# Row loads of k and v, a conv along the free axis, and a 128-row first transform stage in a two-headed SSM kernel

## The chip, the cores and the metric

The kernel runs on one core of one Trainium2 chip. The time is what the device needs for one execution, in microseconds; of several runs the median is given. The engines are named as in the profile: PE (TensorE matmul; PEld its weight loads), DVE (VectorE), ACT (ScalarE), POOL (GpSimd) and SP (SyncE, which issues most DMAs). Each engine takes its instructions in the order in which they stand in its own stream.

## The reference

Two sequence mixers over 2048 steps, with 640 channels each, stand side by side in the output. A is a diagonal complex state-space model, B a gated long convolution.

```python
# A: per step t
Lam_bar = exp(dt * Lam);  B_bar = ((Lam_bar - 1) / Lam)[:, None] * Bmat
h = Lam_bar * h + x[t] @ B_bar.T
y = 2 * (hs @ Cmat.T).real + x * Dskip
# B
k_shift = sum(k_pad[:, t:t+S] * shift_k[:, 3 - t] for t in range(4))   # causal, 4 taps
kv = k_shift * v
y = irfft(rfft(kv, 4096) * rfft(ssm_k, 4096))[:2048] + kv * ssm_D
out_B = q * y
out = concat([out_A, out_B])          # (1, 2048, 1280), bfloat16
```

## The kernel before

Everything lives in one SBUF arena of 128 partitions (class `Layout` gives each named part its columns; parts are reused in time) and in eight PSUM banks. `build` (L947) describes the program as a list of operations with the arena columns that each reads and writes; `Program.depend` makes dependencies of these. The order of the work is not found at run time: the string `ORDER` (L1050) holds one entry per operation, its number, the letter of its engine (T = PE, A = ACT, V = DVE, G = POOL, S = SP) and its PSUM bank. So an operation such as an eviction, an addition or a scaling that could run on several engines runs on the one that its entry names, and a wait holds up all that stands behind it on that engine. The numbers of the operations are given out in the order of `build`, so a change of the program gives all entries new numbers.

Part A works on time cut into 16 residues (i) of 128 steps (s). The *up* sweep (`up2`, `up1`, `up0`, matmuls at L554 through `base` and L575 through `rmm`) multiplies transposed x (`load_x`, L522, eight DMA transposes) with transposed B (`load_B`, L489) and combines residues in a tree; it is evicted at L571, L595 and L620. `coarse` (L646 to L660, names cs_...) runs the scan over the 128 coarse steps. `scale_C` (gC, L544, evicted at L548) scales the output matrix. `down` (dn, L677 and L679, evicted and added at L695 or L697, names ad...) distributes the states: where the addition runs on DVE it is a tensor addition of PSUM and SBUF, where it runs on ACT, PE adds the old value with an identity matmul first (L677) and ACT only copies. `project` (C, L714) makes the output: it loads the rows of x (L705), multiplies them with Dskip (xd, L706), adds the product in PSUM (ev_C, L716) and stores (st_A, L720). In these names the digits behind a stage are the unit, for instance the level and the first channel block.

Part B is a transform of length 4096 in two stages, on half of the channels (hf 0 or 1, 320 channels) at a time. Time is split in 32 coarse steps a and 64 fine steps b; the partitions hold (e, a), with four groups e of 80 channels. The filter ssm_k is h, its load `load_h` (L762) and `addD` (L764, which adds ssm_D into the filter's first column, for which a small load of ssm_D, ld_D, must have landed). The first stage `s1` (L832, evicted at L837, names e1...) has ten units of eight channel columns for h and for k, per half: each 64-row half of the partitions is multiplied by the table F1, in tiles of 64 rows by 64 columns, four at a time. The second stage `s2` (L850, evicted at L863, e2...) multiplies with the table W. `product` (L874 to L881; pp, pq, py, pz) multiplies the two spectra; `r2` (L895, L900) and `r1` (L916, and L928, which multiplies with q) transform back; `store` (L940) writes out. `tables_G` (L327, L329; g_q, g_s, g_k) makes the table for `r1`.

What k and v go through before the first stage is this. `load_kv` (L769) loads k and v of 128 channels by a DMA transpose each, with channels on the partitions and time along the free axis, five times (d = 0 to 4). `conv` multiplies the shifted k with a scalar per partition (cm, four times, by the helper at L197 or L198, on DVE or ACT), adds (ca, L795, three times) and multiplies with v (cx, L796). `plane` (L802) spills the result to a DRAM tensor, kv_rows, and `relay` (L812) reloads it with (e, a) on the partitions, four DMAs per half, each in runs of 64 elements. `setup` fills the tables: F1 at L271; `load_small` loads the four shift weights of each channel (L745).

The call of the first stage, for column i of a unit, half b of the table and half l of the rows:

```python
e.matmul(B[64 * b:64 * b + 64, 512 * l + 64 * i:512 * l + 64 * i + 64], lhsT=lh[i][ps], rhs=F[ps, b, :], start=True,
         stop=True, tile_position=(64 * l, 64 * b))
```

## Time and profile before

| | us |
|---|---|
| median of 3 runs (206.31 to 207.75) | 206.9 |
| span of the profiled execution | 205.6 |
| first matmul of the up sweep | 10.67 |
| mean granted TensorE clock | 0.970 of full speed |

In the profile a row of grouped instructions reads: line, engine, operation, what it writes and reads, the shapes, the count; then the busy time in us and the mean of one in ns; then the idle time of the engine in front of them, and what ended it. A row of a stretch reads: its bounds, its length, the busy time of each engine with the number of instructions in brackets, the granted clock, the share of the 16 DMA engines that was busy, and what they moved. A row of a wait reads: who waited, for whom, how long in all, how often, the longest. A row in order of time reads: start, length, engine, line, operation, count. A busy PE is not a PE at its peak: the end of a matmul is modelled, and two that overlap are one busy stretch. A DMA share can read a little over 1.

The DMA queues took 77.4% of the time of the 16 engines, in 107226 packets of 29.35 MB, nearly all of them under 512 bytes. The DMAs that the change is about, KB each and median us from issue to landing (none where the landing isn't seen):

```profile
arena<-in_B_ssm_k_dram SPq DMA_DIRECT2D x8, 320.0 KB, 7.1
kv_rows<-arena SPq DMA_DIRECT2D x5, 512.0 KB, 4.2
arena<-in_B_k_dram SPq DMA_TRANSPOSE x5, 5.7
arena<-in_B_v_dram SPq DMA_TRANSPOSE x5
```

### The profile page before, as it was taken

To read this page: it belongs to the slowest core of one execution; us is meant where nothing else is said; L and a number is where in the kernel's file an instruction comes from. 1 tells how busy PE (TensorE), PEld (TensorE's weight loads), DVE (VectorE), ACT (ScalarE), POOL (GpSimd) and SP (SyncE) were. 2 spreads that over 40 slices of the span, in tenths; PEclk is the share of its full clock that TensorE was granted. 3 is DMA by queue.
4 is the path that set the end of the run, shared out by engine and by line. 5 is a ranking of instruction groups with operands and counts; after the bars stand their busy time and mean duration, and the time that the engine had idled before them with its cause. 6 is when DMAs were issued, how large, how long until landed. Compare 5 with 4: busy or idle time off the path is not lost.

```text
span 205.6 us, 8247 instructions
## 1 busy us (share of the span) xinstructions
PE 180.7 (88%) x3713; PEld 118.7 (58%) x3713; DVE 166.2 (81%) x228; ACT 142.5 (69%) x164; POOL 76.4 (37%) x63
## 2 busy tenths in 40 slices
PE   2399999999999989768759999999999998999891
PEld 0245444554556647447546757546577776887670
DVE  4929349798949698798697989999999899988821
ACT  2628897887994889999738799996999950550000
POOL 8799900000040727037310180684910507120120
PEclk9999999999999999999965899999999999999998
DMA  4999979989999989659948990140962794166866
GB/s 124 160 195 168 183 163 168 136 187 156 228 222 180 267 135 199 109 100 129 134 141 171 161 101 3 40 129 3 212 80 67 171 218 96 66 160 168 227 165 156
DMA packets 107549, 30.20 MB, mean 147 GB/s; under 512 B 102394, under 2 KB 106874, under 8 KB 107514
## 3 DMA queue, kind: packets, MB, share of 16 engines
q1 hardware_dynamic: 107226, 29.35, 77.4%
q8 instruction: 29, 0.48, 1.1%
q10 hardware_dynamic: 288, 0.33, 0.5%
q14 instruction: 6, 0.05, 0.1%
HBM read 10.99 MB, written 7.86 MB: 92 GB/s over the span
## 4 chain that ended last, share of the span: by engine, by line
PE 46%; ACT 24%; DVE 10%; DMA 10%; issue 5%; POOL 1%; SPq 0%; DVEq 0%; ACTq 0%
PE acc L714 14%; PE acc L554 12%; ACT arena L863 8%; ACT arena L837 7%; DMA arena<-in_B_k_dram 6%; PE acc L850 5%; PE acc L679 3%; PE acc L832 3%; PE acc L895 3%; DVE arena L716 2%; PE acc L575 2%; DVE arena L874 2%; ACT arena L198 2%; DVE arena L877 2%; PE acc L916 2%
## 5 line engine op out<-in xcount | busy, mean ns | idle before, releaser
L554 PE MATMUL acc<-arena 128*64 128x512 bf16 x400 | 50.0, 403 | 3.9 <-issue 3.6
L714 PE MATMUL acc<-arena 128*128 128x320 bf16 x320 | 46.0, 300 | 1.4 <-DVE arena L716 0.8
L554 PEld LDWEIGHTS <-arena 128*64 128x64 bf16 x400 | 23.4, 112 | 26.5 <-issue 6.5
L714 PEld LDWEIGHTS <-arena 128*128 128x128 bf16 x320 | 30.4, 98 | 14.4 <-issue 0.9
L837 ACT CAST arena<-acc 128x1024 bf16<-128x1024 f32 x34 | 32.7, 1033 | 5.8 <-PE acc L832 5.6
L863 ACT CAST arena<-acc 128x960 bf16<-128x960 f32 (+1 forms) x37 | 32.5, 907 | 5.7 <-PE acc L850 4.9
L850 PE MATMUL acc<-arena 128*64 128x160 bf16 x512 | 23.2, 238 | 2.5 <-ACT arena L863 1.3
L832 PE MATMUL acc<-arena 64*64 64x64 bf16 x1280 | 18.2, 205 | 6.9 <-ACT arena L837 3.0
L706 POOL TENSOR_TENSOR arena<-arena 128x640 bf16<-128x640 bf16 x9 | 13.4, 1499 | 28.0 <-DMA arena<-in_A_x_dram 28.0
L850 PEld LDWEIGHTS <-arena 128*64 128x64 bf16 x512 | 18.2, 111 | 8.8 <-ACT arena L863 3.7
L900 ACT CAST arena<-acc 128x1024 bf16<-128x1024 f32 x16 | 15.5, 1021 | 10.8 <-PE acc L895 10.8
L832 PEld LDWEIGHTS <-arena 64*64 64x64 bf16 x1280 | 14.5, 117 | 14.0 <-ACT arena L837 6.2
L795 DVE TENSOR_TENSOR arena<-arena 128x2048 bf16<-128x2048 bf16 x14 | 17.8, 1268 | 5.8 <-ACT arena L198 5.5
L198 ACT ACTIVATE arena<-arena 128x2048 bf16<-128x2048 bf16 (+3 forms) x15 | 18.6, 1243 | 5.4 <-DMA arena<-in_B_k_dram 4.2
L697 DVE TENSOR_TENSOR arena<-acc,arena 128x1024 bf16<-128x1024 f32 (+2 forms) x17 | 19.2, 1148 | 1.4 <-ACT arena L863 0.7
L881 POOL TENSOR_TENSOR arena<-arena 128x1280 bf16<-128x1280 bf16 x3 | 8.5, 2821 | 27.5 <-DVE arena L877 27.5
L716 DVE TENSOR_TENSOR arena<-acc,arena 128x640 bf16<-128x640 f32 x16 | 13.3, 832 | 4.9 <-PE acc L714 4.8
L434 POOL TENSOR_TENSOR arena<-arena 128x1280 bf16<-128x1280 bf16 x1 | 2.3, 2331 | 32.1 <-ACT arena L198 32.1
L679 PE MATMUL acc<-arena 128*128 128x512 bf16 (+2 forms) x50 | 13.0, 346 | 0.6 <-ACT arena L837 0.5
L197 DVE TENSOR_SCALAR arena<-arena 128x2048 bf16<-128x2048 bf16 (+2 forms) x17 | 11.8, 699 | 1.2 <-DMA arena<-in_B_k_dram 0.9
L928 DVE TENSOR_TENSOR arena<-acc,arena 128x960 bf16<-128x960 f32 (+1 forms) x12 | 11.9, 1040 | 0.7 <-DMA arena<-in_B_q_dram 0.4
L874 DVE TENSOR_TENSOR arena<-arena 128x2560 bf16<-128x2560 bf16 x8 | 11.9, 1486 | 0.1
(139 smaller groups left out, 269.1 us busy)
## 6 DMA issues: line engine op xcount, KB each, us to landing
out_dram<-arena SPq DMA_DIRECT2D x32, 160.0 KB, 3.1
arena<-in_B_ssm_k_dram SPq DMA_DIRECT2D x8, 320.0 KB, 7.1
kv_rows<-arena SPq DMA_DIRECT2D x5, 512.0 KB, 4.2
arena<-kv_rows SPq DMA_DIRECT2D x8, 320.0 KB, 5.6
arena<-in_A_x_dram SPq DMA_DIRECT2D x16, 160.0 KB, 4.2
arena<-in_B_q_dram SPq DMA_DIRECT2D x8, 320.0 KB, 5.7
arena<-in_A_B_im_dram ACTq DMA_DIRECT2D x1, 160.0 KB
arena<-in_A_B_re_dram ACTq DMA_DIRECT2D x1, 160.0 KB, 2.7
```

Of the source, the lines that this page charges most:

```text
L198: self.SM = {nc.scalar: lambda out, in_, by: nc.scalar.mul(out, in_, by), nc.vector: vm(nc.vector), nc.gpsimd: vm(nc.gpsimd)}
L554: e.matmul(o[64 * r:64 * r + 64], lhsT=self.BT[j][:, r, d, :], rhs=self.XP[:, d, 2 * q:2 * q + 2], start=(d == 0), stop=(d == 4), skip_gro ...
L679: e.matmul(B[:, o:o + 128 * k], lhsT=c.RR[:, n, j, :], rhs=A[:, j, q:q + k, 0:128], start=not by_pe, stop=True, skip_group_check=True)
L697: e.tensor_tensor(out=o, in0=b, in1=o, op=ALU.add)
L714: e.matmul(B[:, 512 * b:512 * b + 320], lhsT=lh[j], rhs=self.CT[:, j, 320 * b:320 * b + 320], start=(j == 0), stop=(j == 9))
L716: P.add(f"ev_C{i}", {PDVE: dve(640)}, lambda e, B: e.tensor_tensor(out=ys.rearrange("p (b n) -> p b n", b=2), in0=B.rearrange("p (b n) -> ...
L795: P.add(f"ca{d}_{j}", tt, lambda e: e.tensor_tensor(out=t1, in0=t1, in1=t2, op=ALU.add), outs=[t1], ins=[t1, t2])
L832: e.matmul(B[64 * b:64 * b + 64, 512 * l + 64 * i:512 * l + 64 * i + 64], lhsT=lh[i][ps], rhs=F[ps, b, :], start=True, stop=True, tile_pos ...
L837: P.add(f"e1{what}{hf}_{u}", {PACT: act(1024), PDVE: dve(1024)}, lambda e, B: c.CP[e](out=out, in_=B.rearrange("p (l n k s) -> p k s l n", ...
L850: e.matmul(B[64 * s:64 * s + 64, 512 * b + 160 * i:512 * b + 160 * i + 160], lhsT=c.W[:, k, 64 * b:64 * b + 64], rhs=self.AS[hf][:, k, 160 ...
L863: c.CP[e](out=out, in_=b.rearrange("p r (k j n) -> p r k j n", k=n, j=4) if nj > 1 else b.rearrange("p r (k x) -> p r k x", k=n))
L874: P.add(f"pp{hf}", n1, lambda e: e.tensor_tensor(out=pt, in0=X, in1=Yk, op=ALU.mult), outs=[pt], ins=[X, Yk])
```

## The change

k and v of one half are loaded directly, 16 DMAs in all, with (e, a) on the partitions and, along the free axis, 64 time steps b of 80 channels: runs of 160 bytes. One buffer K, with 240 columns in front for the three time steps before, and the one buffer KV, which v is loaded into, serve both halves. DMA transposes of k and v, kv_rows, `plane` and `relay` are gone. The conv now shifts k by whole rows of 80 columns; the three earlier time steps that lie in another partition are fetched by one matmul with a shift matrix SH (hl) and one copy (ev_hl) per half. The weight of a tap is no longer a scalar per partition but a row of 80 values, repeated over 32 time steps, so each tap is a tensor by tensor multiplication, of 2560 columns, twice per half. The weights are loaded four times over all partitions (ld_sk) and rearranged (sw). The first stage takes all 128 rows at once: F1 has four slots of which one per partition group is filled (me4), and a unit is 16 matmuls of 128 rows with 128 columns, in two column tiles. Three parameter loads and the weight loads stand on ACT's queue. Some parts of the arena move.

```diff
-for _name, _n in (..., ("Y", 10240), ("T", 6656), ("KT", 2064), ("VT", 6144), ("H0", 5120), ("KV", 5120), ..., ("F1", 128), ...
+for _name, _n in (..., ("Y", 10240), ("T", 2560), ("TT", 5120), ("K", 5360), ("KV", 5120), ("H0", 5120), ..., ("F1", 256), ...
...
+    P.add("iota_sh", {G: .3}, lambda e: e.iota(SH, pattern=[[1, 128]], base=-1, channel_multiplier=-1, ...
+    P.add("sh", {V: .2}, lambda e: e.tensor_single_scalar(out=SH, in_=SH, scalar=0.0, op=ALU.is_equal), outs=[SH], ins=[SH])
+    edge = SH.rearrange("p (e a) -> p e a", a=32)[:, :, 0:1]
+    P.add("shz", {V: .1, G: .2}, lambda e: e.memset(edge, 0.0), outs=[edge])
...
+    P.add("me4", {V: .12}, lambda e: e.tensor_tensor(out=me4, in0=io4, in1=bc(pe_i, [128, 4]), op=ALU.is_equal), ...
-        out=F1.rearrange("p (k s) -> p k s", s=2), in0=bc(..., [128, 64, 2]), in1=bc(me..., [128, 64, 2]), op=ALU.mult)
+        out=F1.rearrange("p (k s) -> p k s", s=4), in0=bc(..., [128, 64, 4]), in1=bc(me4..., [128, 64, 4]), op=ALU.mult)
...
-        P.add("ld_par", {PSP: .1}, ...
+        P.add("ld_par", {PSP: .1, PACT: .1}, ...
...
+        for x in range(4):
+            rows = raw[32 * x:32 * x + 32]
+            P.add("ld_sk", {PSP: .4, PACT: .4}, lambda e, x=x, rows=rows: e.dma_start(
+                out=rows.rearrange("p (h y) -> p h y", h=2), in_=bass.AP(ssk.tensor, 320 * x, [[0, 32], [1280, 2], [1, 320]])), ...
...
-    def load_kv(self, d):
-        for n, out, x in (("k", c.v("KT", 16, 2048), self.k2), ("v", c.v("VT", 2048 * (d % 3), 2048), self.v2)):
-            P.add(f"ld_{n}{d}", {PSP: 2.3}, lambda e, out=out, x=x: e.dma_start_transpose(out=out, in_=x[:, 128 * d:128 * d + 128]), ...
+    def load_kv(self, hf):
+        for n, out, x in (("k", self.K[:, 240:5360], self.k2), ("v", self.KV, self.v2)):
+            for e_ in range(4):
+                c0 = 320 * hf + 80 * e_
+                d = out[32 * e_:32 * e_ + 32]
+                src = x.rearrange("(a b) d -> a b d", b=64)[:, :, c0:c0 + 80]
+                P.add(f"ld_{n}{hf}_{e_}", {PSP: 2.1}, lambda e, d=d, src=src: e.dma_start(
+                    out=d.rearrange("p (b n) -> p b n", n=80), in_=src), outs=[d], nbytes=32 * 64 * 160)
...
-        def tap(out, j):
-            k, w = c.v("KT", at - j, 2048), c.SW[:, 4 * d + j:4 * d + j + 1]
-            P.add(f"cm{d}_{j}", {PDVE: .7, PACT: act(2048)}, lambda e: c.SM[e](out, k, w), outs=[out], ins=[k, w])
-        tap(t1, 3)
-        for j in (2, 1, 0):
-            tap(t2, j)
-            P.add(f"ca{d}_{j}", tt, ...)
-        P.add(f"cx{d}", tt, ...)
-    def plane(self, d): ...
-    def relay(self, hf): ...
+        last, edge = self.K[:, 5120:5360], self.K[:, 0:240]
+        P.add(f"hl{hf}", {PPE: .11}, lambda e, B: e.matmul(B[:, 0:240], lhsT=c.SH, rhs=last, start=True, stop=True), ...
+        P.add(f"ev_hl{hf}", {PACT: act(240), PDVE: dve(240)}, lambda e, B: c.CP[e](out=edge, in_=B[:, 0:240]), outs=[edge], group=g)
+        tt = {PDVE: dve(2560, .52), PPOOL: 5.1}
+        for q in range(2):
+            Vt = self.KV[:, 2560 * q:2560 * q + 2560]
+            def tap(out, j):
+                k = self.K[:, 240 - 80 * j + 2560 * q:2800 - 80 * j + 2560 * q]
+                w = c.SW[:, hf, j:j + 1, :]
+                P.add(f"cm{hf}_{q}_{j}", tt, lambda e: e.tensor_tensor(out=w3(out), in0=w3(k), in1=bc(w, [128, 32, 80]), op=ALU.mult), ...
+            tap(t1, 3)
+            for j in (2, 1, 0):
+                tap(t2, j)
+                P.add(f"ca{hf}_{q}_{j}", tt, ...)
+            P.add(f"cx{hf}_{q}", tt, ...)
...
-            lh = [self.KV[:, x, :] for x in gs]
+            lh = [self.KV.rearrange("p (b n) -> p n b", n=80)[:, x, :] for x in gs]
             for i in range(8):
                 for b in range(2):
-                    for l in range(2):
-                        ps = slice(64 * l, 64 * l + 64)
-                        e.matmul(B[64 * b:64 * b + 64, 512 * l + 64 * i:512 * l + 64 * i + 64], lhsT=lh[i][ps], rhs=F[ps, b, :], ...
+                    e.matmul(B[64 * b:64 * b + 64, 128 * i:128 * i + 128], lhsT=lh[i], rhs=F[:, b, :], start=True, stop=True,
+                             tile_position=(0, 64 * b))
```

The order is new as a whole. Counted by engine, the operations that can stand on several engines move like this:

| operations | before | after |
|---|---|---|
| cm (tap multiplications) | DVE 14, ACT 6, of 2048 columns | DVE 16, of 2560 |
| ca (tap additions) | DVE 14, POOL 1 | DVE 11, POOL 1 |
| cx (times v) | DVE 5 | DVE 4 |
| e1, e2 (evictions of the two first stages) | ACT 71, DVE 16 | ACT 75, DVE 12 |
| ad (additions of down) | ACT 4, DVE 17 | ACT 10, DVE 11 |
| gC evictions | ACT 8, DVE 2 | ACT 10 |
| g_k (scalings of G) | ACT 5, DVE 2, POOL 1 | ACT 8 |
| xd (x times Dskip) | DVE 7, POOL 9 | DVE 10, POOL 6 |
| pq, py, pz (products) | DVE 24, POOL 8 | DVE 25, POOL 7 |

In the order of SP, loads of the first k half now stand between the last loads of x, all four v loads follow the first h loads, and the loads of the second k half stand behind both loads of C; those of the second v half stand among the h loads of the second half. On DVE the second half's conv stands between the scan of part A and the first products.

More of the change, by code (lines that the diff above doesn't have):

```diff
@@ L985, in build @@
         a.down(0, (j,))
-    for d in range(3):
-        b.load_kv(d)
-        b.conv(d)
-        b.plane(d)
-    b.relay(0)
+    b.load_kv(0)
+    b.conv(0)
     for u in range(10):
```

89 lines of the change are left out of this document (38 added, 51 removed), and 72 rows, old and new, of the table ORDER.

## The prediction

> **What bounds the kernel now.** I read the page's shares first, then the busy time of each engine stretch by stretch, then the waits of the slackest stretch, then durations.
>
> ```profile
> PE 180.7 (88%) x3713; PEld 118.7 (58%) x3713; DVE 166.2 (81%) x228; ACT 142.5 (69%) x164; POOL 76.4 (37%) x63
> ```
> ```profile
> core 0: us, PE busy (x) PEld busy (x) DVE busy (x) ACT busy (x) POOL busy (x), PEclk, DMA share, GB/s
> 0.00:10.70 10.70, 2.99 (x17) 1.68 (x19) 7.77 (x40) 5.37 (x8) 8.42 (x24) 1.00 0.78 144
> 10.70:78.20 67.50, 65.60 (x1006) 36.37 (x1008) 49.91 (x71) 53.32 (x65) 22.03 (x20) 1.00 1.08 184
> 78.20:136.60 58.40, 49.01 (x1460) 34.43 (x1455) 52.04 (x55) 49.74 (x57) 23.85 (x10) 0.91 0.68 118
> 136.60:200.20 63.60, 62.12 (x1236) 45.97 (x1236) 55.65 (x63) 34.05 (x37) 22.11 (x12) 1.00 0.60 133
> ```
> ```profile
> 104.00:114.00 10.00, 8.43 (x307) 6.24 (x311) 8.82 (x11) 6.88 (x8) 0.00 (x0) 0.54 0.57 132
> ```
>
> The share of 88% hides four stretches. I cut them at the first matmul of the up sweep (10.7), the first eviction of filter stage two (78.2), the end of the last first-stage unit (136.6) and the last projection (200.2). In the second, PE is busy 65.6 of 67.5 us although the DMA engines are full (1.08): there the k and v transposes cost PE almost nothing. The fourth is PE's too, 62.1 of 63.6. Only the third, which I call the middle, has room: PE 49.0, DVE 52.0, ACT 49.7 of 58.4. In it lie the filter's second stage, all other first-stage units, s2k0, three projections and most of "down": short matmuls, each followed by an eviction of about 1 us on ACT or DVE.
>
> ```profile
> ACT arena L837 <- PE acc L832: 4.2, 5, 2.2
> PE acc L832 <- DVE arena L764: 2.4, 1, 2.4
> DVE arena L764 <- DMA arena<-in_B_ssm_D_dram: 1.5, 1, 1.5
> ```
>
> One hole in the middle is a DMA's: addD1 (L764) waits 1.5 us for its small load, PE then stands 2.4 us, and from 104 to 114 runs at a granted clock of 0.54, while ACT waits for it.
>
> So taking DMA work away frees an engine that holds up little; what counts is what the change does to PE in stretches two and four, and to the evicting engines in the middle.
>
> **Part by part.** *Head.* PE starts on the up sweep when the x transposes have landed.
>
> ```profile
> 0.94 0.41 SPq L346 DMA_DIRECT2D arena<-in_A_Lambda_im_dram  x1
> 1.41 0.29 SPq L346 DMA_DIRECT2D arena<-in_A_log_dt_dram  x1
> 1.75 0.33 SPq L346 DMA_DIRECT2D arena<-in_A_Lambda_re_dram  x1
> ...
> 3.74 0.58 SPq L745 DMA_DIRECT2D arena<-in_B_shift_k_dram  x1
> ```
>
> These four issues leave SP ahead of the needed transposes: 0.41 + 0.29 + 0.33 + 0.58 = 1.6 us. The transposes ahead stay as many (one of B, two of x). They go to ACT's queue, with three more for the repeated shift weights; ACT is busy 5.4 of these 10.7 us, which hides them. If it doesn't, up to that 1.6 is lost instead. I take -1.5.
>
> *Direct loads.* Ten transposes, five spills and eight reloads go; sixteen row loads come.
>
> ```profile
> arena<-kv_rows SPq DMA_DIRECT2D x8, 320.0 KB, 5.6
> ```
>
> The nearest row, the reload of the same 320 KB in 128-byte runs, took 5.6 us to land; the new runs have 160 bytes. The first half comes long before DVE reaches its conv. There is one K buffer: the second k half waits on SP for the last multiply of the first conv, the second v half for the last k unit of half 0. Behind them on SP stand the residual rows of x and the last h load, for which xd1, addD1 and s1h1 wait. Between DVE's last eviction of those k units and the first product with v stand fourteen DVE instructions, so I cost it at 0; without that cover, at what a load takes beyond them, up to 3.
>
> *First stage.* A unit was 32 matmuls of 64 rows and 64 columns, four at a time; it becomes 16 of 128 rows and 128 columns, two at a time. PE has that shape already in L575.
>
> ```profile
> 44.34 0.75 PE L832 MATMUL acc<-arena 64*64 64x64 bf16 x64
> 45.02 2.45 PE L554 MATMUL acc<-arena 128*64 128x512 bf16 x20
> ...
> 59.13 1.01 PE L575 MATMUL acc<-arena 128*64 128x128 bf16 x24
> 59.98 2.43 PE L554 MATMUL acc<-arena 128*64 128x512 bf16 x20
> ```
>
> Two old units take 45.02 - 44.34 = 0.68, so 0.34 each. New: (59.98 - 59.13) / 24 = 0.035 per matmul, 0.57 a unit; or, if it runs at the rate of L554 (20 of 512 columns in 2.45, so 0.031 for 128 columns), 0.49. So +0.15 to +0.23 a unit. Ten lie in stretch two, on PE's path: +1.5 to +2.3, I take +1.9, as both rows are near. Thirty lie in the middle: up to 6.9 us of PE. [...]
>
> *The middle.* I compared both orders between the first eviction of s2h0 and the last of s1k1.
>
> ```profile
> L863 ACT CAST arena<-acc 128x960 bf16<-128x960 f32 x22 | 20.8, 967 | 3.1 <-PE acc L850 2.6 <-ACT arena L620 0.2
> L697 DVE TENSOR_TENSOR arena<-acc,arena 128x1024 bf16<-128x1024 f32 x7 | 8.4, 1220 | 0.8 <-ACT arena L863 0.7
> L863 DVE CAST arena<-acc 128x960 bf16<-128x960 f32 x6 | 6.9, 1154 | 1.0 <-PE acc L850 0.5 <-ACT arena L620 0.4
> L874 DVE TENSOR_TENSOR arena<-arena 128x2560 bf16<-128x2560 bf16 x4 | 6.0, 1488 | 0.1
> L877 DVE TENSOR_TENSOR arena<-arena 128x1280 bf16<-128x1280 bf16 x7 | 5.5, 821 | 0.2
> L863 ACT CAST arena<-acc 128x640 bf16<-128x640 f32 x4 | 2.8, 692 | 0.1
> ```
> ```profile
> L795 DVE TENSOR_TENSOR arena<-arena 128x2048 bf16<-128x2048 bf16 x14 | 17.8, 1268 | 5.8 <-ACT arena L198 5.5
> L197 DVE TENSOR_SCALAR arena<-arena 128x2048 bf16<-128x2048 bf16 x14 | 10.7, 768 | 1.1 <-DMA arena<-in_B_k_dram 0.9
> L796 DVE TENSOR_TENSOR arena<-arena 128x2048 bf16<-128x2048 bf16 x5 | 6.1, 1220 | 0.0
> L434 DVE TENSOR_TENSOR arena<-arena 128x1280 bf16<-128x1280 bf16 x4 | 6.0, 1521 | 0.0
> L548 ACT CAST arena<-acc 128x640 bf16<-128x640 f32 x8 | 5.2, 703 | 0.2 <-PE acc L544 0.2
> L329 ACT ACTIVATE arena<-arena 128x1024 bf16<-128x1024 int32 x4 | 4.3, 1078 | 0.0
> L706 DVE TENSOR_TENSOR arena<-arena 128x640 bf16<-128x640 bf16 x7 | 3.3, 487 | 1.7 <-DMA arena<-in_A_x_dram 1.7
> L695 ACT CAST arena<-acc 128x1024 bf16<-128x1024 f32 x2 | 2.0, 1012 | 1.1 <-PE acc L679 1.1
> L620 ACT CAST arena<-acc 128x256 bf16<-128x256 f32 x5 | 1.9, 387 | 0.3 <-PE acc L575 0.3
> L863 DVE CAST arena<-acc 128x640 bf16<-128x640 f32 x2 | 1.6, 814 | 0.4 <-PE acc L850 0.4
> ```
>
> DVE gains nearly the whole second half of the conv, 15 products and sums of 2560 columns (the 16th sum goes to POOL): 15 x 1.488 = 22.3. It loses two multiplies, two sums and a product of 2048 (2 x 0.768 + 2 x 1.268 + 1.220 = 5.3), five adds of 1024 (6.1), one eviction of 960 (1.2), three of 640 (2.4), one product of 1280 (0.8), and gains two xd (1.0): +7.5, so 59.5. What DVE sheds lands on ACT: three adds of 1024 (3 x 1.012), one of 640 and one more filter-scale eviction (2 x 0.703), one more eviction of 960 (0.967) and two of 640 (2 x 0.692), two sines for G (2 x 1.078), and one short copy more (0.387): +9.3, so 59.0. Each add moved to ACT costs PE an identity matmul.
>
> ```profile
> 143.61 1.55 PE L679 MATMUL acc<-arena 128*128 128x512 bf16 x6
> 145.00 2.88 PE L714 MATMUL acc<-arena 128*128 128x320 bf16 x20
> ```
>
> At (145.00 - 143.61) / 6 = 0.23 each, nine more make +2.1 on PE; six of "down" leave for stretch four, -1.4. PE: 49.0 + 6.9 + 2.1 - 1.4 = 56.6.
>
> So all three would need 57 to 59.5 us where the middle lasts 58.4. Without any idle time it lasts as long as DVE needs, 59.5 (+1.1); at DVE's present share of 52.04 / 58.40 = 0.89, 66.8 (+8.4). The hole at 104 goes, since both D loads now go out early; but three full engines feed each other here. I take half way, 63.2: +4.8.
>
> *Stretch four.* The six matmuls arrive: +1.4. The evictions and products there stay; the G scalings that leave DVE and POOL for ACT find ACT at 34.1 of 63.6.
>
> *Sum.* -1.5 + 1.9 + 4.8 + 1.4 = +6.6 on the profiled 205.6, so 212.2; the median of the runs, 206.9, lies 1.3 above the span, which I keep: 213.5.
>
> **Rivals.** *It closes up (faster).* In DVE's new order two multiplies of the second conv stand ahead of its first s2h0 eviction. DVE is busy 49.9 of 67.5 in stretch two; if K comes free early enough they run there, 3.0 us leave the middle, and PE's 56.6 becomes its bound. The hole is gone with the late D load, so the middle lasts just that: -1.8. ACT no longer multiplies in stretch two, evictions come at once and PE's idle there (67.5 - 65.6 = 1.9) pays for the dearer units; the six matmuls fill stretch four's idle (63.6 - 62.1 = 1.5). With the head: -1.5 - 1.8 = -3.3, about 203.5. It decides if the middle closes to under 2 us of idle on PE. For it: ACT's wait of 4.2 behind the hole. Against: three engines without any wait on each other, where the best now has 0.89.
>
> *A wash.* As the forecast, but with the two multiplies ahead of a middle that then lasts as long as now: +6.6 - 4.8 = +1.8, less up to 1.9 for the idle in stretch two, 207 to 208.5.
>
> *Broadcast multiply at half rate.* The shift weights are now a tensor repeated over 32 rows of time. L434, the row with repeated operands, takes 1.521 for 1280 columns, 1.19 ns each, where L874 takes 0.58. If the multiplies went so, each would take 3.0 instead of 1.49, eight in the middle add 12 and replace most of the idle: about 222. Against: L434 also reads a 32-bit operand. [...]
>
> **How the numbers follow.** 1% is 2.1 us, about what this kernel's runs tell from no change. Forecast 0.55 (its own range 209 to 219: the middle at +1.1 or +8.4, a head without its gain, a first-stage unit at either price); it closes up 0.17; a wash 0.18; half-rate multiply 0.10. Faster 0.17, same 0.18, slower 0.65. The range reaches from half of the closing case to the upper bounds: 204 to 219.
>
> **What would show it.** Right: the up sweep starts near 9; DVE and ACT are both over 90% busy between the first s2h0 eviction and the last s1k1 one, which lasts 61 to 66 us; the multiplies take 1.5 us; first-stage units 0.45 to 0.57; no stretch at a clock near 0.5 behind addD1. Wrong: a middle under 60 us, multiplies near 3 us, or PE waiting for a k, v or h load.

## The result and the profile after

The changed kernel takes 228.5 us (median of four runs, 227.8 to 229.6) where the kernel before takes 207.1 beside it: a ratio of 1.1075, with a 95% interval of 1.1008 to 1.1142. Slower was forecast, but 6.6 us slower; it is 21.4, and the time lies above the whole range. The profiled execution has a span of 227.8 us, and the busy shares of the page:

```profile
PE 201.9 (89%) x3087; PEld 141.6 (62%) x3091; DVE 172.1 (76%) x220; ACT 136.7 (60%) x171; POOL 67.0 (29%) x57
```

PE is 21 us busier, in fewer matmuls than before. The stretches by the prediction's own cuts (first matmul of the up sweep, first eviction of filter stage two, end of the last eviction of a first-stage unit, last projection); the columns are bounds, length, busy time of PE, PEld, DVE, ACT and POOL, granted clock, DMA share and GB/s:

```profile
0.00:16.30 16.30, 3.10 (x17) 1.66 (x18) 2.19 (x19) 2.51 (x2) 7.91 (x22) 1.00 0.94 180
16.30:84.20 67.90, 66.49 (x850) 38.22 (x851) 52.83 (x81) 40.06 (x64) 22.62 (x19) 1.00 0.99 126
84.20:158.60 74.40, 67.30 (x980) 55.06 (x981) 57.58 (x55) 57.82 (x68) 15.60 (x6) 0.91 0.51 74
158.60:223.90 65.30, 64.16 (x1242) 46.33 (x1240) 58.64 (x65) 36.34 (x39) 20.86 (x11) 1.00 0.49 115
```

Against 10.7, 67.5, 58.4 and 63.6 before: head +5.6, stretch two +0.4, the middle +16.0, stretch four +1.7, and the end behind it 1.5 shorter; together the 22.2 us between the spans. So two places hold the loss.

The head, in order of time (start, length, engine, line, operation):

```profile
4.83 0.11 DVE L351 MEMSET arena<- 128x64 uint32 x1
...
7.54 0.53 ACTq L354 DMA_DIRECT2D arena<-in_A_Lambda_re_dram  x1
11.09 0.29 ACTq L354 DMA_DIRECT2D arena<-in_A_Lambda_im_dram  x1
12.57 0.29 ACTq L354 DMA_DIRECT2D arena<-in_A_log_dt_dram  x1
...
16.13 0.19 PE L362 MATMUL acc<-arena 128*128 128x30 bf16 x1 [6.91 <-DMA arena<-in_A_log_dt_dram]
16.28 1.06 PE L562 MATMUL acc<-arena 128*64 128x512 bf16 x4
```

The three parameter loads, on SP at 0.9 to 2.1 us before, are issued by ACT between 7.5 and 12.9. They need the memset of their tile (L351), which the new order puts behind other work on DVE, at 4.83; before, it stood first there, at 0.80. The little matmul that turns the parameters (t_par, now L362) is the third operation in PE's order; it stands until the last load has landed at 16.1, and the up sweep (now L562) stands behind it.

The first-stage units (now L838), PE's matmuls in order of time: five h units, the ten k units of half 0, three h units of half 1, and the ten k units of half 1:

```profile
55.32 2.63 PE L838 MATMUL acc<-arena 128*64 128x128 bf16 x80
92.54 13.07 PE L838 MATMUL acc<-arena 128*64 128x128 bf16 x160 [0.38 <-ACT arena L869]
122.46 1.53 PE L838 MATMUL acc<-arena 128*64 128x128 bf16 x48 [0.49 <-ACT arena L869]
139.48 5.27 PE L838 MATMUL acc<-arena 128*64 128x128 bf16 x64
149.61 7.90 PE L838 MATMUL acc<-arena 128*64 128x128 bf16 x96
```

An h unit of 16 matmuls takes 2.63 / 5 = 0.53 us, a k unit 13.07 / 10 = 1.31: 33 and 82 ns a matmul in the same shape. Both evicting engines now wait for PE there (the first two rows):

```profile
L843 ACT CAST arena<-acc 128x1024 bf16<-128x1024 f32 x34 | 33.4, 1029 | 18.6 <-PE acc L838 18.5
L843 DVE CAST arena<-acc 128x1024 bf16<-128x1024 f32 x6 | 7.3, 1222 | 8.9 <-PE acc L838 8.9
L815 DVE TENSOR_TENSOR arena<-arena 128x2560 bf16<-128x2560 bf16 x16 | 23.7, 1489 | 0.5 <-ACT arena L805 0.2
```

The third row is the tap multiplication: 1.49 us, not the 3.0 of the half-rate rival; a product of as many columns without a repeated operand takes the same (L880, 1488 ns). What differs between the two kinds of unit is the weight: 64 neighbouring columns of H, or 64 columns of KV that lie 80 columns (160 bytes) apart. The granted clock falls in the k units, but the pace doesn't follow it (bounds, length, busy time of PE and PEld for these matmuls alone, clock, DMA share, GB/s; a matmul that reaches over a bound is counted on both sides of it):

```profile
94.00:96.00 2.00, 2.00 (x30) 2.00 (x28) 1.00 1.58 128
100.00:102.00 2.00, 2.00 (x30) 2.00 (x28) 0.50 0.04 8
```

The ten k units of half 0, over half of their time at a clock of 0.50, take 13.07 us; those of half 1, at 0.94 to 1.00, take 5.27 + 7.90 = 13.17.

### The profile page after: what moved, and what is told of

Read it like the earlier page. It is cut to its first block, busy times and chain, and to the rows that moved or that the text cites. A ratio compares the mean times of both kernels' runs of the same rounds, so it can differ in the third digit from the quotient of the medians.

```text
span 227.8 us, 6977 instructions
## 1 busy us (share of the span) xinstructions
PE 201.9 (89%) x3087; PEld 141.6 (62%) x3091; DVE 172.1 (76%) x220; ACT 136.7 (60%) x171; POOL 67.0 (29%) x57
## 4 chain that ended last, share of the span: by engine, by line
PE 56%; DVE 17%; ACT 8%; DMA 7%; SPq 5%; issue 3%; POOL 1%; DVEq 0%; ACTq 0%; POOLq 0%
PE acc L562 21%; PE acc L838 12%; PE acc L722 11%; ACT arena L869 5%; DMA arena<-in_B_v_dram 4%; PE acc L583 3%; PE acc L901 3%; DVE arena L880 3%; ACT arena L556 2%; DVE arena L934 2%; DMA arena<-in_A_x_dram 2%; DVE arena L820 2%; SPq L530 2%; PE acc L856 2%; SPq L785 2%
## 5 line engine op out<-in xcount | busy, mean ns | idle before, releaser
L562 PE MATMUL acc<-arena 128*64 128x512 bf16 x400 | 49.8, 403 | 0.0
L722 PE MATMUL acc<-arena 128*128 128x320 bf16 x320 | 47.7, 306 | 0.3 <-ACT arena L843 0.3
L843 ACT CAST arena<-acc 128x1024 bf16<-128x1024 f32 x34 | 33.4, 1029 | 18.6 <-PE acc L838 18.5
L838 PE MATMUL acc<-arena 128*64 128x128 bf16 x640 | 37.2, 279 | 2.4 <-ACT arena L843 1.5
L838 PEld LDWEIGHTS <-arena 128*64 128x64 bf16 x640 | 35.5, 190 | 4.3 <-ACT arena L843 1.7
L562 PEld LDWEIGHTS <-arena 128*64 128x64 bf16 x400 | 23.7, 112 | 22.4 <-issue 2.9
L869 ACT CAST arena<-acc 128x960 bf16<-128x960 f32 (+1 forms) x41 | 35.6, 911 | 2.9 <-PE acc L856 2.4
L856 PEld LDWEIGHTS <-arena 128*64 128x64 bf16 x512 | 17.8, 109 | 10.2 <-ACT arena L869 3.5
L815 DVE TENSOR_TENSOR arena<-arena 128x2560 bf16<-128x2560 bf16 x16 | 23.7, 1489 | 0.5 <-ACT arena L805 0.2
L906 ACT CAST arena<-acc 128x1024 bf16<-128x1024 f32 x15 | 14.6, 1015 | 10.5 <-PE acc L901 10.4
L724 DVE TENSOR_TENSOR arena<-acc,arena 128x640 bf16<-128x640 f32 x16 | 13.0, 818 | 9.6 <-PE acc L722 9.5
L887 POOL TENSOR_TENSOR arena<-arena 128x1280 bf16<-128x1280 bf16 x3 | 8.4, 2789 | 28.5 <-DVE arena L883 23.3
L820 DVE TENSOR_TENSOR arena<-arena 128x2560 bf16<-128x2560 bf16 x11 | 16.5, 1502 | 0.2
L843 DVE CAST arena<-acc 128x1024 bf16<-128x1024 f32 x6 | 7.3, 1222 | 8.9 <-PE acc L838 8.9
L885 POOL TENSOR_TENSOR arena<-arena 128x1280 bf16<-128x1280 bf16 x1 | 3.7, 3748 | 34.9 <-DVE arena L883 34.9
L705 DVE TENSOR_TENSOR arena<-acc,arena 128x1024 bf16<-128x1024 f32 x11 | 13.0, 1215 | 0.9 <-PE acc L687 0.9
L880 DVE TENSOR_TENSOR arena<-arena 128x2560 bf16<-128x2560 bf16 x8 | 11.9, 1488 | 1.6 <-ACT arena L869 1.4
L579 ACT CAST arena<-acc 128x1024 bf16<-128x1024 f32 x6 | 6.1, 1012 | 11.4 <-PE acc L562 11.4
L901 PE MATMUL acc<-arena 64*128 64x128 bf16 x320 | 12.1, 226 | 0.2 <-POOL arena L883 0.2
```

The source lines that it names most:

```text
L562: e.matmul(o[64 * r:64 * r + 64], lhsT=self.BT[j][:, r, d, :], rhs=self.XP[:, d, 2 * q:2 * q + 2], start=(d == 0), stop=(d == 4), skip_gro ...
L722: e.matmul(B[:, 512 * b:512 * b + 320], lhsT=lh[j], rhs=self.CT[:, j, 320 * b:320 * b + 320], start=(j == 0), stop=(j == 9))
L815: P.add(f"cm{hf}_{q}_{j}", tt, lambda e: e.tensor_tensor(out=w3(out), in0=w3(k), in1=bc(w, [128, 32, 80]), op=ALU.mult), outs=[out], ins=[ ...
L820: P.add(f"ca{hf}_{q}_{j}", tt, lambda e: e.tensor_tensor(out=t1, in0=t1, in1=t2, op=ALU.add), outs=[t1], ins=[t1, t2])
L838: e.matmul(B[64 * b:64 * b + 64, 128 * i:128 * i + 128], lhsT=lh[i], rhs=F[:, b, :], start=True, stop=True, tile_position=(0, 64 * b))
L843: P.add(f"e1{what}{hf}_{u}", {PACT: act(1024), PDVE: dve(1024)}, lambda e, B: c.CP[e](out=out, in_=B.rearrange("p (n k l s) -> p k s l n", ...
```

## The experiments

Each ratio is to the kernel before, run beside it on the same chip. Some of the tables and runs stand on different chips, so that times from different places are compared by their ratios. The edits are to the changed kernel unless said.

**One loss undone at a time.** x_head_sp moves one memset and three loads to the front of the order, x_k_contig changes one line, x_both has both, and x_h1_step gives the h units of half 1 the k units' step.

```diff
-"... 28V0 52V0 ... 143S0 53A0 127T4 54A0 55A0 57T7 ..."
+"52V0 53S0 54S0 55S0 88V0 18G0 ... 143S0 127T4 57T7 ..."                      # x_head_sp, x_both
-            lh = [self.KV.rearrange("p (b n) -> p n b", n=80)[:, x, :] for x in gs]
+            lh = [self.KV.rearrange("p (n b) -> p n b", b=64)[:, x, :] for x in gs]   # x_k_contig, x_both
+            if hf == 1: H = self.h[hf].rearrange("p (b g) -> p g b", g=80)             # x_h1_step
```

> The changed kernel, with the memset of the parameter tile and its three small loads first in the order and on SP's queue, as they were before; nothing else moves. Theory A (the loss in the head: the three loads sit on ACT's queue, are issued at 7.5, 11.1 and 12.6 us, and PE, which takes its work in order, stands at t_par until 16.1): the up sweep starts between 10.5 and 12 instead of 16.3, and the time falls by 4 to 5.5, to 223 to 224.5. Rival B (the up sweep waits for the transposes of B and x, t_par is only the last name on it): the start moves by less than 1 us and the time by less than 1, 227.5 to 228.5.

> The changed kernel, whose k units read their weights as 64 neighbouring columns of KV instead of 64 columns 80 apart; so the first stage of k takes the wrong columns, and the same amount of them. Theory A (the weight loads with a step of 160 bytes take 82 ns each and nothing hides them): a k unit falls from 1.31 us to the 0.50 of the h units, the twenty give back up to 16.2, PE in the middle no longer ends last, and the time is 212 to 214. Rival B (the shape of 128 rows and 128 columns is itself dear when it follows short matmuls): the k units stay above 1.2, the time within 1 of 228.5. Rival C (ACT and DVE, which evict, hold the middle as the prediction had it): the units get short but the evictions end last, the middle falls only to 66 to 68 and the time to 220 to 222.

> Both edits at once: parameter loads first on SP, and the k units' weights as neighbouring columns (wrong columns for k). Theory A (two independent losses): 228.5 - 5 - 15.5 = 207 to 209.5, with the up sweep from about 11 and a middle of about 58 to 61. Rival C (evictions hold the middle): 215 to 217. If the gain of the two is less than the sum of the two single ones by over 1.5 us, the head's loss was partly hidden behind a later wait.

> The changed kernel, whose ten h units of the second half read their weights 80 columns apart as the k units do (so other columns for that half). H is written by loads long before, and no conv runs on it. Theory A (the step of the weights sets the time of a unit): these units go from about 0.50 to 1.3 us each, 8 us more on PE; they lie in the middle among evictions, which hide at most 2 of it: 234 to 237. Rival D (k units are slow because DVE writes or loads fill KV at the same time, or because their data come late): the h units stay at 0.50, time within 1 of 228.5.

| run | us | ratio (95% interval) | theory |
|---|---|---|---|
| x_head_sp | 222.9 | 1.0686 (1.0601 to 1.0771) | A, not B |
| x_k_contig | 212.2 | 1.0164 (1.0097 to 1.0230) | A; neither B nor C |
| x_both | 208.4 | 0.9996 (0.9957 to 1.0035) | A, not C |
| x_h1_step | 234.6 | 1.1230 (1.1144 to 1.1317) | A, not D |

In x_head_sp the up sweep starts at 10.43; then it is a load of x that PE waits for. In x_both the k units run at the h units' pace, and the loss of the change is gone. PE's matmuls of x_both in order of time, nine of the ten k units of half 0 (4.62 us where ten took 13.07):

```profile
86.64 4.62 PE L838 MATMUL acc<-arena 128*64 128x128 bf16 x144 [0.35 <-ACT arena L869]
```

The stretches of x_both by the same cuts:

```profile
0.00:10.10 10.10, 2.99 (x17) 1.69 (x18) 3.00 (x22) 2.51 (x2) 7.29 (x21) 1.00 0.71 154
10.10:77.30 67.20, 65.89 (x851) 39.46 (x851) 54.31 (x78) 40.08 (x64) 22.63 (x21) 0.97 0.96 148
77.30:135.80 58.50, 49.32 (x981) 36.91 (x981) 56.71 (x55) 56.22 (x68) 15.37 (x5) 1.00 0.66 94
135.80:201.80 66.00, 64.34 (x1242) 46.41 (x1240) 59.47 (x66) 36.32 (x39) 20.83 (x11) 1.00 0.48 114
```

Within this series the step costs 222.9 - 208.4 = 14.5 us and the head 212.2 - 208.4 = 3.8: the sweep starts 6 us sooner, and 2 of them are lost again further on (stretch four lasts 65.3 us in x_k_contig and 67.1 in x_both, both cut at the last first-stage matmuls). x_head_sp moves the memset and the queue together, so it doesn't tell how much of the head belongs to which. In x_h1_step ten h units take 13.0 us, although their data come from loads long before and nothing writes H beside them: it is the step, not how KV is filled.

**What a step costs.** y_steps adds groups of matmuls behind the end, which change no result.

```diff
+    w = lambda i, n, st: A[:, lo(i):lo(i) + (n - 1) * st + 1:st]          # A: a tile that holds data
+    [e.matmul(B[64 * b:64 * b + 64, ...], lhsT=w(i, 64, 80), rhs=F[:, b, :], start=True, stop=True, tile_position=(0, 64 * b)) for i in range(16) for b in range(2)]
```

> The changed kernel with a block added behind its last matmul that changes no result: 20 groups of matmuls whose weights are 64 (or 128) columns of a tile at a step of 1, 2, 4, 8, 16, 32, 40, 64, 80, 82, 96, 128 or 160 columns of 2 bytes, each group behind 14 full matmuls. First the form of the new unit (128 rows, 64 columns, twice per weight, 128 columns of data), then the old unit's four tiles of 64 by 64 at steps 1 and 80, then 64 rows by 128 columns (the form of r2) at 1, 40 and 80, then 128 by 128 at 1 and 80. The k units of the changed kernel took 82 ns a matmul at step 80, its h units 31 at step 1. Theory A1 (what costs is that no two neighbouring columns lie in the same 16 bytes): 31 to 35 ns at steps 1, 2 and 4, 75 to 90 at every step from 8 on. Theory A2 (any step above 1 costs the same): 75 to 90 from step 2 on. Theory A3 (certain steps collide, 80 among them): a saw-tooth, with 82 or 40 far cheaper than 80. For the old form at step 80: if loads of different rows run side by side, 4 tiles take about as long as one, 20 to 25 ns a matmul; if not, 75 to 90.

In order of time, the new unit's form at steps 1, 4, 8, 80, 82 and 96; the old form's four tiles at 1 and 80; then 64 rows by 128 columns at 1, 40 and 80:

```profile
228.26 1.08 PE L1043 MATMUL acc<-arena 128*64 128x128 bf16 x32
...
236.55 1.18 PE L1047 MATMUL acc<-arena 128*64 128x128 bf16 x32
...
240.79 2.12 PE L1049 MATMUL acc<-arena 128*64 128x128 bf16 x32
...
266.72 2.77 PE L1059 MATMUL acc<-arena 128*64 128x128 bf16 x32
...
272.55 2.67 PE L1061 MATMUL acc<-arena 128*64 128x128 bf16 x32
...
278.28 2.00 PE L1063 MATMUL acc<-arena 128*64 128x128 bf16 x32
...
294.01 0.71 PE L1069 MATMUL acc<-arena 64*64 64x64 bf16 x64
...
297.78 2.75 PE L1071 MATMUL acc<-arena 64*64 64x64 bf16 x64
...
303.59 1.07 PE L1073 MATMUL acc<-arena 64*128 64x128 bf16 x32
...
307.72 1.20 PE L1075 MATMUL acc<-arena 64*128 64x128 bf16 x32
...
311.98 1.50 PE L1077 MATMUL acc<-arena 64*128 64x128 bf16 x32
```

From the first start to the last, over 31, the groups give 28 ns a matmul at steps 1 and 2 (about (1.08 - 0.22) / 31, as the last matmul itself takes 0.22 us, like the h units' 219 ns; at step 8 0.28 and at step 80 0.32 are taken off, where the k units of half 1 have 323 ns), 31 at 4, 59 at 8, 60 at 16 and 40, 56 at 32, 96 and 160, 63 at 64, 73 at 128, 76 at 82 and 79 at 80. So the break is where A1 puts it, between 8 and 16 bytes, but above it the price is not one price; 80 is the dearest of those tried. A1's reason, whether two neighbouring columns lie in the same 16 bytes, was the author's guess: it agrees with the break (31 ns at 8 bytes, 59 at 16), no run shows it by itself, and it gives no reason for the spread from 56 to 79. The old form at step 80 takes 39 ns a matmul (8 at step 1), 32 x 39 = 1.2 us a unit: the tiles of 64 rows would have been no way out. Weights of 128 columns on 64 rows, two groups of rows in turn, bear the step far better: 28, 32 and 41. All this is from one execution, whose mean granted clock was 0.953; the groups of full matmuls in between keep one pace, 2.97 to 3.20 us each.

**What closing the step costs.** y_turned stores the product k x v channel by channel, so that the weights are neighbours; z_forms measures forms of writing; v_fours stores groups of four channels.

```diff
-            P.add(f"cx{hf}_{q}", ..., e.tensor_tensor(out=Vt, in0=t1, in1=Vt, op=ALU.mult), ...
+  o = R.rearrange("p (n b) -> p b n", b=64)[:, 32 * q:32 * q + 32]                 # y_turned
+  o = R.rearrange("p (m b r) -> p b m r", b=64, r=4)[:, 32 * q:32 * q + 32]        # v_fours
+  e.tensor_tensor(out=o, in0=cut(t1), in1=cut(Vt), op=ALU.mult)    # half 0: R = XT[5120:]; half 1: R = H0
+  e.tensor_copy(out=o, in_=cut(V0))                                # half 1, first product: turned afterwards
```

> A version that computes what it should: the parameter loads first on SP, and k for the first stage stored channel by channel, so that its weights are neighbouring columns. For the first half the two last products of the conv write their result with a step of 64 columns into a part of XT that is free then; for the second half the first product goes to POOL in place and a POOL copy turns it into H0 behind the h units, and the second writes into H0 itself; the loads of q that want H0 move behind the k units. With a strided write a product of 2560 columns should lose DVE's double rate, 2.7 us instead of 1.49 (estimate: 1.04 ns a column, the rate of DVE's evictions). Against x_both's 208.4: DVE in the middle, 55.6 of 57.4 us there, loses one product of 1.5 and gains 1.2. Theory A (the weights' step and the head were the losses): 207.5 to 210.5. Rival (the strided writes or POOL's work hold DVE up, or s1k1 waits for POOL's copy): 211 to 215, with PE idle ahead of s1k1.

It takes 258.8 us, 1.2515 (1.2468 to 1.2563). The rival, and far beyond its price. The 2.7 us for a product written with a step was the author's estimate, from the pace of DVE's evictions (before, 1222 ns for 1024 columns at L837 and 421 for 256 at L620: 1.04 for each column more); no run shows such a product at that pace. The two writes with a step, groups of y_turned (busy us, mean ns, idle before):

```profile
L831 DVE TENSOR_TENSOR arena<-arena 128x2560 bf16<-128x2560 bf16 x3 | 35.1, 11712 | 1.0 <-PE acc L857 1.0
L839 POOL COPY arena<-arena 128x2560 bf16<-128x2560 bf16 x1 | 22.5, 22507 | 14.3 <-ACT arena L862 14.3
```

POOL's 22.5 us is not the price of its copy alone: the copy starts at 142.15, when one of the DVE products with a step is under way (from 142.0 on, for at least 11.6 us), and no run has such a copy by itself.

> The changed kernel with sixteen operations of 128x2560 added behind its end, one after the other, that change no result: DVE products written as they are read, then in runs of 1, 2, 4, 8 and 16 neighbouring columns (2 to 32 bytes), then read with a step of 80 columns and written without a gap; DVE copies read with that step, and written in runs of 4; ACT copies plain, in runs of 1 and 4, and read with the step; POOL copies plain, in runs of 4 and read with the step. In y_turned a product written in runs of 1 took 11.6 us where the plain one takes 1.5, and POOL's copy 22.5. Theory W1 (a write costs per run, 4.5 ns each on DVE): 5.8 at runs of 2, 2.9 at 4, 1.5 at 8. Theory W2 (what costs is only that a write is narrower than 16 bytes or so): near 11 up to runs of 4, near 1.5 to 2.7 from 8 on. Reading with the step: if reads cost like writes, 11 or more; if a step costs a read only the double rate, 2.7.

In order of time: DVE's product plain, in runs of 1, 2 and 4, and read with the step; a copy read with the step, and one written in runs of 4; ACT's copy plain and in runs of 1:

```profile
222.80 1.48 DVE L1045 TENSOR_TENSOR arena<-arena 128x2560 bf16<-128x2560 bf16 x1
224.32 11.54 DVE L1046 TENSOR_TENSOR arena<-arena 128x2560 bf16<-128x2560 bf16 x1
235.90 2.32 DVE L1047 TENSOR_TENSOR arena<-arena 128x2560 bf16<-128x2560 bf16 x1
238.26 1.49 DVE L1048 TENSOR_TENSOR arena<-arena 128x2560 bf16<-128x2560 bf16 x1
...
242.84 5.13 DVE L1051 TENSOR_TENSOR arena<-arena 128x2560 bf16<-128x2560 bf16 x1
248.00 2.65 DVE L1052 COPY arena<-arena 128x2560 bf16<-128x2560 bf16 x1
250.68 0.83 DVE L1053 COPY arena<-arena 128x2560 bf16<-128x2560 bf16 x1
251.54 2.32 ACT L1054 COPY arena<-arena 128x2560 bf16<-128x2560 bf16 x1 [45.41 <-DVE arena L1053]
253.90 11.57 ACT L1055 COPY arena<-arena 128x2560 bf16<-128x2560 bf16 x1
```

Neither W1 nor W2: single columns cost 4.5 ns each, on DVE and on ACT; pairs cost 2.32 us for 1.48; runs of four cost nothing (1.49 us). A read with the step costs less than a write of single columns: DVE's product 5.13 us against 11.54.

> A second version that computes what it should: parameter loads first on SP, and k for the first stage stored in groups of four channels, so that a weight's 64 columns lie 4 columns (8 bytes) apart and a product writes runs of 4. Where the results go is as in y_turned (a free part of XT for the first half, H0 for the second, one of its two products turned by a POOL copy). z_forms: a product in runs of 4 takes 1.49 us as the plain one, POOL's copy 2.3; y_steps: 31 ns a matmul at step 4 against 28 at step 1. So it should cost what x_both cost: 0.99 to 1.01 of the kernel before; the k units 0.45 to 0.56 us, and no product of the conv over 1.6 us. Rival (POOL's copy holds up DVE or the first k unit of the second half): 1.01 to 1.03, with PE waiting for POOL.

It takes 216.3 us, 1.0444 (1.0380 to 1.0508): the rival, though the products take 1.48. Beside POOL's copy a DVE product of 0.8 us takes 2.94, and PE later stands 5.8 us behind an addition of DVE whose residual row came late.

> v_fours with its two suspected faults undone: the copy that turns the first product of the second half goes from POOL, where it took 3.4 us and stretched the DVE product beside it from 0.8 to 2.9, to DVE, where runs of 4 took 0.83; and the four loads of q, which stood on SP ahead of the residual rows of x, move in two pairs behind the loads of the other q. If the first alone counted: 1.01 to 1.03 of the kernel before; if the loads of q did (in v_fours PE stands 5.8 us behind an addition that DVE makes late, and loads of x are 6% of its chain): 0.995 to 1.01 with both undone.

211.2 us, 1.0170 (1.0132 to 1.0208). By the ratio it is the first case, as if the loads of q didn't count. But the wait of 5.8 us is gone, and another has come, of 3.0 us for a DVE addition (L724) behind the last product, which now meets POOL's next sum:

```profile
118.98 3.07 POOL L902 TENSOR_TENSOR arena<-arena 128x1280 bf16<-128x1280 bf16 x1 [27.77 <-DVE arena L900]
119.50 3.90 DVE L829 TENSOR_TENSOR arena<-arena 128x2560 bf16<-128x2560 bf16 x1
```

In v_fours the same two meet too, but there the product starts first, and it is the sum that takes long:

```profile
120.65 1.48 DVE L829 TENSOR_TENSOR arena<-arena 128x2560 bf16<-128x2560 bf16 x1
120.87 3.73 POOL L902 TENSOR_TENSOR arena<-arena 128x1280 bf16<-128x1280 bf16 x1 [0.82 <-DVE arena L900]
```

> v_fours_2 with the copy and the last product of the second half's conv ahead of the DVE product that releases POOL's; in v_fours_2 that last product took 3.9 us instead of 1.48 while POOL worked on a sum beside it. If that meeting is what was left of the loss: the product takes 1.5, and the ratio falls from 1.017 to 1.003 to 1.010 (the copy's 0.8 us stays). If not: 1.013 to 1.020.

208.5 us, 1.0041 (1.0001 to 1.0082), as expected; the product takes 1.49 and the copy 0.83. So the whole computation with direct loads and close weights gives back nearly the whole loss, and is no faster than the kernel before.

**What holds the middle.** Five runs look for what sets its length once the step is gone; y_before_D asks what the hole in the kernel before was worth.

```diff
-  in0=w3(k), in1=bc(w, [128, 32, 80])     +  in0=w3(k)[:, 0:m], in1=bc(w, [128, m, 80])   # y_light, on x_both: m = 1 for taps 0 and 1 of half 1, the sums alike
-  "... 466A0 ... 461A0 ..."               +  both behind the last e1k1 entry of ACT        # z_sines: two g_s, on x_both
-  "... 494A6 ... 488A0 ... 490A0 ..."     +  494V6, 488V0, 490V0                         # z_light_evict, on y_light with z_sines: h evictions 5, 2, 3 to DVE
-  "... 490A0 ... 486A6 ... 492A4 ..."     +  490V0, 486V6, 492V4, and 432V0 412V0 behind 411V0   # w_chains, on the same: h evictions 3, 1, 4, the conv's end first
-  "... 680T2 ... 681V2 682S0 698S0 ..."   +  ahead of 314T2                                # w_three, on the same: second projection
-  "... 438T6 411V0 436T4 117S0 ..."       +  "... 116S0 117S0 ..."                         # y_before_D, on the kernel before
```

> x_both (parameter loads first, k's weights as neighbouring columns, which are the wrong ones) that leaves out nearly all of two taps of the second half's conv: four products and four sums work on 80 columns instead of 2560, some 8 x 1.3 = 10 us less of DVE, seven of them in the middle. In x_both the middle lasts 57.4 us with DVE busy 55.6, ACT 55.1 and PE 48.2. Theory E1 (DVE alone sets the middle, as the prediction's sum had it): the middle falls by 7 to 9 to PE's 48 to 50, and the time to 200 to 201. Theory E2 (ACT is as full, so taking DVE's load gives only what ACT waited for): the middle falls by 1 to 3, the time to 205.5 to 207.5.

> x_both (parameter loads first, k's weights as neighbouring columns, the wrong ones) with the two sines of G that ACT makes in the middle, 1.08 us each, moved on ACT behind the last eviction of the k units; nothing else. y_light took 9.6 us of DVE out of the middle and it stayed at 57.4 us. Theory E3 (ACT alone sets the middle): it falls by about 2 to 55.3, the time from 208.4 by 1.5 to 2. Theory E4 (DVE, at 55.6 of 57.4, takes over at once): by less than 1. Theory E5 (the middle is set by PE's order and its waits, not by a full engine): no change.

> y_light (which leaves out nearly all of two taps of the second half's conv, so DVE has 46 of 57.4 us in the middle) with the two sines moved as in z_sines and three evictions of the second half's h units given from ACT to DVE: ACT falls from 55.5 to about 50.3, DVE rises to 49.6, PE needs 48.5. Theory E3 (ACT alone sets the middle, and DVE has room here): the middle falls to 51 to 53, the time from 207.3 to 201.5 to 203. Theory E5 (PE's order and its waits): within 1.5 of 207.3.

> y_light (which leaves out nearly all of two taps of the second half's conv) with the two sines of G moved behind the middle as in z_sines, and the second projection, 2.9 us of PE that stand between the last h unit and filter stage two, moved behind eight units of that stage with its addition and its store. Taken alone, the DVE work (y_light) and the sines (z_sines) changed nothing. Theory E6 (three chains meet near 119 us at the first filter eviction, which overwrites what the conv's last product read: the end of the conv on DVE, the projection on PE, a sine on ACT; each covers the others): only without all three does filter stage two begin 2 to 3 us earlier, the middle falls from 57.4 to 54.5 to 55.5 and the ratio to the kernel before to 0.985 to 0.993, where y_light had 1.004 and z_sines 1.006. Theory E5 (PE's order and its waits elsewhere): within 0.005 of 1.004.

> y_light (which leaves out nearly all of two taps of the second half's conv), the two sines moved as in z_sines, the last product of the conv ahead of the last h evictions on DVE, and the last three of the ten h evictions given from ACT to DVE; the projection stays. In the traces so far filter stage two of the second half starts at 118 to 119 us: it reads what all ten h evictions write, which ACT makes in a row (108.8 to 118.0 in z_sines), and overwrites what the conv's last product reads. Theory E7 (this start holds the middle, and ACT's ten evictions with the projection behind them set it): the first matmul of that stage moves from 118.7 to about 116.5, and the middle shortens by 1.5 to 2.5, the ratio to the kernel before from y_light's 1.004 to 0.990 to 0.998. Theory E5 (PE's order and its waits further on take the gain back): the stage starts earlier, and the ratio stays at 1.000 to 1.008.

| run | us | ratio (95% interval) |
|---|---|---|
| y_light | 207.3 | 1.0037 (1.0009 to 1.0066) |
| z_sines | 209.4 | 1.0060 (1.0024 to 1.0097) |
| z_light_evict | 209.5 | 1.0082 (1.0040 to 1.0123) |
| w_three | 213.8 | 1.0246 (1.0182 to 1.0310) |
| w_chains | 208.0 | 1.0023 (0.9975 to 1.0070) |

The middle of y_light between the cuts of x_both:

```profile
77.30:135.80 58.50, 49.56 (x984) 37.05 (x987) 47.08 (x56) 56.59 (x68) 15.36 (x5) 1.00 0.66 93
```

DVE loses 9.6 us (56.71 to 47.08) and the length stays. From the first eviction of filter stage two to the end of the last of the first stage it is 58.4 us in x_both, 58.0 in y_light. E1 is refuted: DVE's load alone doesn't set the middle. The 207.3 us lie in E2's range, but the ratio shows no gain over x_both. z_sines takes two sines, some 2 us, from ACT, and the middle still lasts 58.3: E3 falls. It can't tell E4 from E5, as DVE is nearly full there; w_chains can, which takes load from both engines and has a middle of the same length:

```profile
77.91:135.80 57.89, 49.35 (x981) 36.91 (x981) 50.13 (x58) 51.61 (x62) 15.35 (x5) 1.00 0.63 94
```

DVE is busy 50.1 us and ACT 51.6, where x_both has 56.7 and 56.2. z_light_evict decides little, since DVE came late to two of its evictions and PE waited 2.6 us for it. w_three and w_chains show that filter stage two of half 1 is ready late from several sides: without the projection PE waits 3.0 us for the last of ACT's ten h evictions; with three of those on DVE, PE still makes the projection from 115.9 to 118.8, and ACT waits 3.57 us in front of that stage. So neither E6 nor E7 as put, and w_three also loses 2% behind the moved projection. Settled is that neither DVE's load nor ACT's sets it, nor the two together; that it is PE's order and its waits (E5) is what is left, not shown by itself, and which order would shorten it was not found.

> The kernel before the change, with its second small D load issued right behind the first, some 50 us earlier on SP; nothing else. It isolates what the prediction counted as the hole: DVE's wait of 1.5 us for that load, PE's of 2.4 behind it, and the stretch at a granted clock of 0.54. If the hole lies on the path: 204.5 to 205.5 against 207 (1.5 to 2.4 less), and no clock near 0.5. If the engines fill each other's gaps there anyway: within 0.7 of the kernel before.

207.2 us, 1.0066 (1.0016 to 1.0116): nothing is gained, and the stretch from 104 to 114 keeps its granted clock of 0.54. The wait only gets another name, the filter's own load (y_before_D; who waited for whom, us in all, times, longest):

```profile
PE acc L832 <- DVE arena L764: 2.4, 1, 2.4
DVE arena L764 <- DMA arena<-in_B_ssm_k_dram: 1.3, 1, 1.3
```

## Why the prediction was wrong

- **First stage, the step that failed.** A unit was priced by L575 and L554, rows with the right shape, and 0.49 to 0.57 us was right for the h units (0.53). But the change also turns the k weights from neighbouring columns into columns 80 apart, one line of the diff, and this was not priced: 1.31 us for each of twenty units, 14.5 us in x_both against x_head_sp. The bound of 6.9 us for thirty units in the middle was thus no bound: their matmuls keep PE busy 14.0 us there before and 31.7 after. The kernel before even had a row with a step, r2 at L895 with 40 columns, and it would have misled: y_steps shows that on 64 rows and 128 columns that step costs little (32 ns a matmul for 28).
- **Head.** "ACT is busy 5.4 of these 10.7 us, which hides them", with 1.6 us as the worst, was wrong: +5.6 us, 3.8 of them at the end. ACT's busy time didn't tell when its queue issues a DMA: busy 2.5 of the 16.3 us, it issued these three at 7.5, 11.1 and 12.6; nor was it asked who stands behind these loads. It is t_par, third in PE's order, and so the up sweep. Nor was the memset looked at: before its end at 4.94 us no queue could have issued these loads, and no run parts its place from the queue. Why ACT then issues them only from 7.5 us on isn't shown; the trace shows SP issuing transposes all that time, and in x_head_sp the second weight load, then first behind ACT's copy, still goes out only at 10.4.
- **The middle, +4.8.** Without the two losses it lasts 58.5 us, as before. The needs were 3 us too high on DVE (59.5, measured 56.7) and ACT (59.0, 56.2) and 7 on PE (56.6, 49.3). Of PE's 7, 5 are the units': a unit that stood alone behind an eviction kept PE busy 0.45 us before, not 0.34 (the thirty 14.0), and in x_both the thirty take 15.9, +1.9 where 6.9 was added. And the busiest engine's share did not stay at 0.89: DVE has 56.7 / 58.5 = 0.97. The hole behind addD1 was misread: y_before_D shows another load behind the one that the row names, and the same clock.
- **Stretch two, +1.9:** x_both has 67.2 us against 67.5; the ten h units keep PE busy 5.5 us for 4.1, the up sweep's main matmuls 48.8 for 50.0. **Stretch four, +1.4:** x_both has 66.0 against 63.6, +2.4, and the end behind it is 1.5 shorter.
- **Direct loads at 0:** right; the one wait that the changed kernel's profile puts down to a k or v load is 0.4 us of DVE, for v (L821).
- **Rivals.** A wash is what x_both comes to, at 1.00. The faster rival needed a middle bound by PE alone; PE stands idle 9 us in that of x_both. The half-rate multiply is refuted by 1.49 us; what makes L434 slower (1.19 ns a column), its 32-bit operand or another thing, no run shows. That DVE and ACT would be over 90% busy in the middle holds for x_both (0.97 and 0.96), not for the changed kernel (57.58 / 74.40 = 0.77).

## What to carry to other kernels

When an operand's layout changes, price the step of its innermost axis as an operation of its own, for who reads it and for who writes it: matmul weights of 64 columns took two to three times as long from a step of 16 bytes on (56 to 79 ns on 128 rows, for 28), and writes of single 2-byte columns eight times on DVE and five on ACT (11.54 us for 1.48, 11.57 for 2.32). A layout with runs of four (8 bytes) satisfied both sides here (31 ns a matmul for 28, 1.49 us a product for 1.48). For a small load that is moved, look at what it waits for and at who stands behind it in the order of the engine that waits for it (here the up sweep, at 16.28 us, behind t_par, at 16.13), not at how busy the new queue's engine is.

## What was not expected of the hardware

- The pace of the k units is the same at a granted clock of 1.00 and of 0.50 (13.17 us for ten units, and 13.07), with PEld busy 2.00 of 2.00 us in both rows: where these weight loads set the pace, the clock didn't.
- Between steps of 16 bytes and more the price of a 64-column weight is uneven: 56 ns at 64, 192 and 320 bytes, 76 and 79 at 164 and 160.
- Where a DVE product and a POOL operation met, the one that started later took longer. In v_fours_2 POOL's sum starts at 118.98 and the product, 0.5 us later, takes 3.90 us; in v_fours the same product starts 0.2 us ahead of the same sum and takes 1.48, and the sum takes 3.73, where such a sum of POOL took 2.61 in the kernel before (L879, at 132.83). The runs of four are not the cause: in x_both a plain tap multiplication that starts 0.15 us behind a POOL product (45.65, 45.50) takes 3.09, and the plain last product, 0.2 us ahead of POOL's sum (117.64, 117.85), takes 1.48. How far this holds for other operations isn't shown.
